# Query loads for two chunks at once, as token pairs in 512-byte rows, with keys turned apart from them

## The chip, the cores and the metric

The kernel runs on one core of one Trainium2 chip. The metric is the device time of one execution in microseconds. Three runs of the kernel before took 303.69, 302.69 and 303.46 us, median 303.46. "PE" in the rows is TensorE, DVE VectorE, ACT ScalarE, POOL GpSimd and SP SyncE, the engine that issues nearly all transfers.

## The reference

A retention layer (attention without softmax, with a decay for each head) feeds a gated feed-forward layer:

```python
# q, k, v: (8 batches, 8 heads, 576 tokens, 64)
scores = matmul(q, k.transpose) / 8
ret = scores * where(row >= col, gamma[head] ** (row - col), 0)
attn = matmul(ret, v)
x = attn.transpose(0, 2, 1, 3).reshape(4608, 512)
gate = sigmoid(x @ w_gate)                # (512, 1536)
out = (gate * (x @ w_val)) @ w_out        # (1536, 512)
```

All inputs and the output are float32; the kernel computes in bfloat16 and sums in float32.

## The kernel before

**Retention by chunks.** The decay is split into a factor of the query's place and one of the key's place, so q and k are scaled by tables (`qtab`, `ktab`) when they are cast to bfloat16. A sequence of 576 tokens is four chunks of 128 tokens and a last one of 64. For a chunk the kernel makes the scores inside it, masks them with the triangle `tri`, multiplies them with v (`intra`), and adds the product of the queries with the running state, the sum of k·v over the chunks before (`inter`). A chunk is worked in two pieces of 64 tokens, `j`. Heads `y*4 + m` lie by halves: `half(y)` is the 64 partitions of one half, `m` one of four positions in a row.

The first six chunks of batches 0 and 1 go through a code of their own (`PAIRS`) that loads two chunks at once as token pairs, in 512-byte rows. The rest are 30 **steps** (`STEPS`), of one chunk each; the last chunks of two batches share a step (6, 11, 20 and 29). `load(s)` issues the loads of k, q and v of a step, in rows of 256 bytes (one head of one token). `cast_qk` scales and casts k and q into one tile `natural_qk[s]`, keys and queries side by side; `cross(s)` turns both by one transposing transfer on SP's queue, and steps 0, 1 and 7 (`TURNED`) are turned on TensorE by `turn_step` instead, with a copy on ACT and one on DVE. `cast_v` makes the values. Scores, state products and values are 64x64 matmuls.

**The feed-forward layer** runs over blocks of columns (tokens): one of 512 for the first pairs, two of 256, then seven of 512. In the blocks of 512 the products are made by a scheme with seven products of quarters for eight, whose operands are sums and differences: of weights (`w_sums`, `wo_sums`), of x (`x_sums`, tile `xsum`) and of the gated values (`gv_sum`, tile `gsum`). These sums run on DVE ("v") or POOL ("p"), as written in the order lists. For this scheme, x lies in the blocks of 512 with even tokens first and odd tokens behind ("dealt"); ACT writes it so from the value banks (`leave_two`, line 788, and line 800).

**Order.** Everything is issued in program order from one list of units: `FIRST`, `ORDER` and `FINAL` are the quarter products of the first, a middle and the last block of 512; a tag such as `0-1v` behind one adds a sum. `LATER*` puts sums beside the products of the output. Between the units, `SUMS_AT` places weight sums, casts (`c`) and turns (`t`) in the form block.unit, `PAIRS_AT` and `next_two` place the bursts of attention, `CASTS_AT` and `LEAD_CAST` the casts of later steps, `AHEAD` says how many steps the loads run ahead of the casts, `EARLY` which gate products of the next block stand among the output products of this one, `SOONER` when stores are issued. `LOOK_ACT`, `K_ON_POOL` and `V_ON_ACT` choose engines by step; from step 11 on (`SCALED_V`) keys are cast without scaling and values are scaled on POOL instead. `CUTS`, `FIRST_OP_CUTS` and `OP_CUTS` say how many 512-column matmuls are issued as two of 256. Each engine works through its own queue in order, SP's queue of transfers too: a transposing transfer there waits for its cast, and the loads behind it with it.

The sum that a DVE row at `L324` shows is a weight sum of the output matrix, `L365` one of gate or value weights, `L829` the addition to the running state, `L658` its cast for the products, `L686` the scores, `L718` and `L734` the value and state products, `L1046` the quarter products, `L1173` and `L1249` those of the output, `L1306` and `L1549` the output of the first three blocks.

Of the kernel before, what the change touches and what calls it, by code (L numbers as in the profile page):

```python
# [16 lines left out]
def kernel(  # L17
# [146 lines left out]

    def load(s):
        b, c = STEPS[s]
        tiles = []
        for nm, src in (("k", k), ("q", q), ("v", v)):
            t = landing([P, H, D], f"{nm}32_{s}", s >= 8)
            if c < LAST:  # L170
                nc.sync.dma_start(out=t, in_=src[b, :, c * P:(c + 1) * P, :].rearrange("h p d -> p h d"))
            else:
                for j, (bj, tj) in enumerate(pieces_of(s)):
                    nc.sync.dma_start(out=t[half(j)], in_=src[bj, :, tj:tj + 64, :].rearrange("h p d -> p h d"))
            tiles.append(t)
        loaded[s] = tiles
# [117 lines left out]
    def later_constants():  # L294

        nc.gpsimd.memset(tri, 1.0)
        for p0 in (0, 64):
            nc.gpsimd.affine_select(out=tri[p0:p0 + 64], in_=tri[p0:p0 + 64], compare_op=ALU.is_ge, fill=0.0,
                                    base=0, pattern=[[1, 64]], channel_multiplier=-1)
# [95 lines left out]

    natural = {}
# [17 lines left out]
    natural_qk = {}  # L414
# [5 lines left out]
    def cast_qk(s, i, eng):  # L420
        c = STEPS[s][1]
        if i == 1:
            natural_qk[s] = nat_pool.tile([P, 2, M, P], BF16, tag="qk", name=f"qk_{s}")
        to = natural_qk[s][:, i].rearrange("p m (y d) -> p y m d", y=2)
        if i == 1 and s >= SCALED_V:
            (on_pool if s in K_ON_POOL else on_act)(out=to, in_=by_halves(loaded[s][0]))
            return
        tab = (qtab, ktab)[i][:, c, :].rearrange("p (y m) -> p y m", y=2).unsqueeze(3).to_broadcast([P, 2, M, D])
        eng.tensor_tensor(out=to, in0=by_halves(loaded[s][1 - i]), in1=tab, op=ALU.mult)  # L429

    SCALED_V = 11
    X_LATE = "ppvp"
    X_FIRST = "vvvp"
    LOOK_ACT = (0, 5, 6, 9, 10, 13, 14, 17, 18, 19, 20, 21, 22, 25, 26, 27, 29, 33, 34)
    K_ON_POOL = (13, 15, 17, 18, 19, 22, 26, 27, 28, 29)
    V_ON_ACT = ()

    def cast_v(s, eng):
        natural["v", s] = nat_pool.tile([P, H, D], BF16, tag="v", name=f"v_{s}", bufs=6)
        if s >= SCALED_V:  # L440
            tab = ktab[:, STEPS[s][1], :].unsqueeze(2).to_broadcast([P, H, D])
            nc.gpsimd.tensor_tensor(out=natural["v", s], in0=loaded[s][2], in1=tab, op=ALU.mult)  # L442
        else:
            eng(out=natural["v", s], in_=loaded[s][2])

    def cross(s):
        t = att_pool.tile([P, 2, M, P], BF16, tag="T", name=f"T_{s}", bufs=6)
        nc.sync.dma_start_transpose(out=t.rearrange("p j m t -> p (j m) t"),
                                    in_=natural_qk[s].rearrange("p j m d -> p (j m d)"))
        turned[s] = t  # L450

    turned = {}

# [24 lines left out]
    def pair_qk(A, g, banks, between=None):  # L478
# [8 lines left out]
        if g == 0:  # L487
            probs["p", A] = [att_pool.tile([P, M, 2, P], BF16, tag="T", name=f"ptp_{A}_{hh}", bufs=6) for hh in range(2)]
# [135 lines left out]
    def turn_step(s):  # L624

        t = att_pool.tile([P, 2, M, P], BF16, tag="T", name=f"T_{s}", bufs=6)
        for i, ((pool, tag), eng) in enumerate(zip(VALS, (on_act, on_dve))):
            ps = pool.tile([P, M, P], BF16, tag=tag, name=f"turn_{s}_{i}")
            for m in range(M):
                nc.tensor.matmul(ps[:, m, :], lhsT=natural_qk[s][:, i, m, :], rhs=ident, is_transpose=True,  # L630
                                 start=(m == 0), stop=(m == M - 1))
            eng(out=t[:, i], in_=ps)
        turned[s] = t
# [47 lines left out]
    def scores(s, begins):  # L681
        t = turned[s]
# [1009 lines left out]
```

## Time and profile before

| | |
|---|---|
| median of three runs | 303.46 us (302.69 to 303.69) |
| profiled execution | 303.89 us, of which the span from first to last instruction 302.2 us |
| TensorE busy | 295.6 us, 98% of the span, granted clock 0.999 |
| weight loads / DVE / ACT / POOL busy | 250.0 / 230.4 / 204.9 / 225.8 us |
| DMA | 54.99 MB in 146,464 packets, 124,400 of them under 512 bytes |
| transfers on SP's queue, as a share of 16 engines | 73.6% |

The busy share of an engine is an average over the whole span. What bounds a stretch is read from the chain of work that ended last, which is followed back from the last instruction: at each step to what released it, or to the instruction before it on its engine. Matmuls overlap, and their ends are modelled, so a row's mean length (273 ns for 256 columns) is longer than the distance between two of them.

### The profile page before, as it was taken

How to read it: one execution, taken by the hardware profiler on the slowest of the kernel's cores; microseconds unless marked ns; L12 is line 12 of the kernel's file. 1: busy time of each engine (PE TensorE's matmuls, PEld its weight loads, DVE VectorE, ACT ScalarE, POOL GpSimd, SP SyncE). 2: the span in 40 equal slices, each digit the busy share in tenths (PEclk: the TensorE clock that was granted, in tenths of full speed). 3: DMA queues.
4: the chain of work that ended last, by engine and by line, in shares of the span. 5: the costliest groups of instructions: out<-in, count | busy, mean ns of one | idle time of the engine just before them, and what ended most of it. 6: DMA issues, size and time to landing. Idle time of an engine off the chain costs nothing.

```text
span 302.2 us, 10696 instructions
## 1 busy us (share of the span) xinstructions
PE 295.6 (98%) x4437; PEld 250.0 (83%) x4437; DVE 230.4 (76%) x439; ACT 204.9 (68%) x414; POOL 225.8 (75%) x253
## 2 busy tenths in 40 slices
PE   7999999999999999999999999999999999999994
PEld 3677876978868888888888888888888888888883
DVE  5967895796986998789748974896489848935893
ACT  6755565335369657985798589857985698559830
POOL 5775854846669888978997898789978946860780
PEclk9999999999999999999999999999999999999999
DMA  7999999979998989999749967976694165004013
GB/s 205 336 370 379 322 334 229 210 160 202 213 175 184 257 173 196 219 201 262 141 108 199 259 143 155 218 185 143 124 204 132 37 123 193 4 2 139 3 36 104
DMA packets 146464, 54.99 MB, mean 182 GB/s; under 512 B 124400, under 2 KB 139760, under 8 KB 146416
## 3 DMA queue, kind: packets, MB, share of 16 engines
q1 hardware_dynamic: 145328, 53.59, 73.6%
q8 instruction: 34, 0.56, 0.8%
q10 hardware_dynamic: 1088, 0.72, 0.8%
q14 instruction: 14, 0.11, 0.1%
HBM read 37.75 MB, written 9.44 MB: 156 GB/s over the span
## 4 chain that ended last, share of the span: by engine, by line
PE 92%; DVE 2%; DMA 2%; issue 1%; ACT 1%; POOL 0%; SPq 0%; DVEq 0%
PE gatea L1046 12%; PE wa L1046 11%; PE qa L1173 11%; PE qe L1173 9%; PE gatee L1046 6%; PE we L1046 5%; PE op L1549 4%; PE h_v L886 3%; PE h_g L886 3%; PE gateg L1046 3%; PE wg L1046 3%; PE hv L1374 3%; PE op L1306 3%; PE val L718 2%; PE qa L1249 2%; PE hg L1374 2%
## 5 line engine op out<-in xcount | busy, mean ns | idle before, releaser
L1046 PEld LDWEIGHTS <-wg_sb 128*128 128x128 bf16 x348 | 34.1, 98 | 4.1
L1073 POOL TENSOR_TENSOR gv<-gv,wu 128x512 bf16<-128x512 bf16 x20 | 23.5, 1174 | 15.5 <-DVE wu L1085 15.4
L1173 PEld LDWEIGHTS <-gsum 128*128 128x128 bf16 x312 | 30.0, 98 | 3.7
L429 POOL TENSOR_TENSOR qk<-q,qtab 128x512 bf16<-128x512 f32 x28 | 30.3, 1082 | 3.5 <-DMA q<-in_q_dram 3.5
L1046 PEld LDWEIGHTS <-wv_sb 128*128 128x128 bf16 x296 | 28.9, 98 | 3.6 <-issue 0.2
L1085 DVE TENSOR_TENSOR gu<-gatee,gu 128x512 f32<-128x512 f32 x22 | 15.2, 690 | 19.4 <-ACT gateg L1077 10.2
L943 POOL TENSOR_TENSOR gsum<-gsum,gv 128x256 bf16<-128x256 bf16 (+1 forms) x20 | 17.6, 890 | 14.4 <-DVE gsum L943 12.6
L1046 PEld LDWEIGHTS <-wgt_sb 128*128 128x128 bf16 x264 | 25.8, 98 | 3.0
L1046 PE MATMUL gatea<-xsum,wg_sb 128*128 128x256 bf16 x172 | 25.6, 273 | 0.0
L1173 PEld LDWEIGHTS <-gv 128*128 128x128 bf16 x228 | 21.8, 98 | 2.7
L1088 DVE TENSOR_TENSOR gs<-gatea,gs 128x512 f32<-128x512 f32 x22 | 15.2, 689 | 9.5 <-PE gatea L1046 9.4
L943 POOL TENSOR_TENSOR gsum<-gv,gsum 128x256 bf16<-128x256 bf16 (+1 forms) x24 | 21.9, 922 | 0.2
L429 POOL TENSOR_TENSOR qk<-k,ktab 128x512 bf16<-128x512 f32 x11 | 11.6, 1054 | 13.4 <-DMA k<-in_k_dram 13.2
L704 DVE TENSOR_TENSOR pt<-row,tri 128x512 bf16<-128x512 f32 x30 | 19.2, 680 | 2.8 <-PE row L686 2.6
L442 POOL TENSOR_TENSOR v<-v,ktab 128x512 bf16<-128x512 f32 x19 | 20.9, 1101 | 0.0
L1046 PE MATMUL wa<-xsum,wv_sb 128*128 128x256 bf16 x136 | 20.4, 273 | 0.1
L658 ACT CAST sb<-s 128x512 bf16<-128x512 f32 (+1 forms) x26 | 14.3, 569 | 8.8 <-DVE s L829 8.7
L788 ACT CAST xT<-val 128x512 bf16<-128x512 f32 x26 | 14.7, 592 | 7.0 <-PE val L734 7.0
L943 DVE TENSOR_TENSOR gsum<-gv 128x512 bf16<-128x512 bf16 (+1 forms) x34 | 19.1, 589 | 0.0
L1046 PEld LDWEIGHTS <-wvt 128*128 128x128 bf16 x168 | 16.4, 98 | 1.9
L943 POOL TENSOR_TENSOR gsum<-gv 128x256 bf16<-128x256 bf16 (+1 forms) x20 | 17.6, 882 | 0.0
L1071 ACT ACTIVATE gv<-gs 128x512 bf16<-128x512 f32 x22 | 13.9, 633 | 5.4 <-DVE gs L1088 5.4
(210 smaller groups left out, 883.9 us busy)
## 6 DMA issues: line engine op xcount, KB each, us to landing
k<-in_k_dram SPq DMA_DIRECT2D x26, 256.0 KB, 3.9
q<-in_q_dram SPq DMA_DIRECT2D x26, 256.0 KB, 4.2
v<-in_v_dram SPq DMA_DIRECT2D x26, 256.0 KB, 4.6
out_dram<-ob SPq DMA_DIRECT2D x24, 256.0 KB, 2.7
wg<-in_moe_w_gate_dram SPq DMA_DIRECT2D x12, 256.0 KB, 5.4
wv<-in_moe_w_val_dram SPq DMA_DIRECT2D x12, 256.0 KB, 5.6
wo<-in_moe_w_out_dram SPq DMA_DIRECT2D x12, 256.0 KB, 5.6
v32p<-in_v_dram SPq DMA_DIRECT2D x6, 256.0 KB, 4.5
```

The lines of the kernel that those rows point to most:

```text
L429: eng.tensor_tensor(out=to, in0=by_halves(loaded[s][1 - i]), in1=tab, op=ALU.mult)
L442: nc.gpsimd.tensor_tensor(out=natural["v", s], in0=loaded[s][2], in1=tab, op=ALU.mult)
L704: nc.vector.tensor_tensor(out=t[:, y, 0:n].rearrange("p i m t -> p (i m) t"), in0=rows_tile[ss[0]][y][:, 0:n].rearrange("p i m t -> p (i m ...
L788: nc.scalar.copy(out=to, in_=src)
L886: nc.tensor.matmul(ps[:, i], lhsT=w_sb[:, kc, (fc + i) * P:(fc + i + 1) * P], rhs=xT(kc, slice(t0, t0 + n)), start=(kc == 0), stop=(kc == ...
L943: eng.tensor_tensor(out=to, in0=a, in1=b, op=op)
L1046: nc.tensor.matmul(ps[:, f], lhsT=w[:, kc, f * P:(f + 1) * P], rhs=x[:, kc], start=(first and f == 0 and kc == 0), stop=(f == 1 and kc == ...
L1073: eng.tensor_tensor(out=to, in0=to, in1=src[:, part], op=ALU.mult)
L1085: nc.vector.tensor_tensor(out=me["u2"], in0=e, in1=me["u2"], op=ALU.add)
L1088: nc.vector.tensor_tensor(out=me["s5"], in0=a, in1=me["s5"], op=ALU.add)
L1173: nc.tensor.matmul(ps[:, b], lhsT=left(fp)[:, b * P:(b + 1) * P], rhs=right(fp), start=(first and fp == 0 and b == 0), stop=(fp == NFC // ...
L1374: nc.tensor.matmul(ps[:, cols], lhsT=(wg_sb if what == "g" else wv_sb)[:, kc, fc * P:(fc + 1) * P], rhs=xT(kc, cols), start=(kc == 0), sto ...
```

## The change

Queries of steps with a whole chunk are loaded for two chunks (256 tokens) by the first step of the two, `opens(s)`, as two tiles of four heads each. A row of a tile holds two neighbouring tokens, 512 bytes. They are scaled by the pair tables (`qtab2`) into one tile of 8 times 128 columns, turned by one transposing transfer (or, for steps 0 and 7, eight transposes), and used by both steps. Keys get tiles of their own and are turned alone, by half the transfer of before.

```diff
+    def opens(s):
+        return STEPS[s][1] < LAST and STEPS[s][1] % 2 == 0
     def load(s):
...
+            if nm == "q" and opens(s):
+                for g in range(2):
+                    t = landing([P, M, 2, D], f"q32_{s}_{g}", s >= 8)
+                    nc.sync.dma_start(
+                        out=t.rearrange("p h r d -> p h (r d)"),
+                        in_=q[b, g * M:(g + 1) * M, c * P:(c + 2) * P, :].rearrange("h (p r) d -> p h (r d)", r=2))
+                    loaded["q", s, g] = t
+            elif nm != "q" or c == LAST:
+                t = loaded[nm, s] = landing([P, H, D], f"{nm}32_{s}", s >= 8)
...
+    def cast_k(s, eng):
+        natural_k[s] = nat_pool.tile([P, M, P], BF16, tag="nk", name=f"nk_{s}", bufs=6)
...
+    def cast_q(s, engs):
+        if c < LAST and not opens(s):
+            return
+        natural_q[s] = nat_pool.tile([P, 2, M, P], BF16, tag="nq", name=f"nq_{s}", bufs=2)
...
+        for g in range(2):
+            tab = qtab2[:, c // 2, g * M:(g + 1) * M, :].unsqueeze(3).to_broadcast([P, M, 2, D])
+            engs[g].tensor_tensor(out=natural_q[s][:, :, :, half(g)].rearrange("p r m d -> p m r d"),
+                                  in0=loaded["q", s, g], in1=tab, op=ALU.mult)
...
     def cross(s):
-        nc.sync.dma_start_transpose(out=t.rearrange("p j m t -> p (j m) t"),
-                                    in_=natural_qk[s].rearrange("p j m d -> p (j m d)"))
+        nc.sync.dma_start_transpose(out=turned_k[s], in_=natural_k[s].rearrange("p m d -> p (m d)"))
+        if q_ is not None and STEPS[s][1] == LAST:
+            nc.sync.dma_start_transpose(out=q_[:, 0], in_=natural_q[s][:, 0].rearrange("p m d -> p (m d)"))
+        elif q_ is not None:
+            nc.sync.dma_start_transpose(out=q_.rearrange("p r m t -> p (r m) t"),
+                                        in_=natural_q[s].rearrange("p r m d -> p (r m d)"))
```

Since even and odd tokens of a chunk now lie apart in the turned queries, a piece of 64 queries is read as two runs of 32 columns, and scores, mask and values keep the order "32 even, 32 odd". The mask `tri` and the reads of the value banks follow from that; in the blocks of 512 the copy to x no longer sorts even from odd, in the blocks of 256 it now mixes them.

```diff
+    def q_of(s, y, m, j):
+        return turned_q[s][half(y), :, m, j * 32:j * 32 + 32]
...
-                    nc.tensor.matmul(row_ps[s][y][half(j), m, :], lhsT=t[half(y), 1, m, half(j)],
-                                     rhs=t[half(y), 0, m, half(j)], ...
+                    nc.tensor.matmul(row_ps[s][y][half(j), m, :].rearrange("p (r t) -> p r t", r=2),
+                                     lhsT=turned_k[s][half(y), m, half(j)], rhs=q_of(s, y, m, j), ...
...
     def turn_step(s):
-        for i, ((pool, tag), eng) in enumerate(zip(VALS, (on_act, on_dve))):
+        sides = [(turned_k[s], natural_k[s], on_dve)]
+        if q_ is not None:
+            sides.insert(0, (q_.rearrange("p r m t -> p (r m) t"), natural_q[s].rearrange("p r m d -> p (r m) d"), on_act))
...
-        src = vals_tile[vals[0]][j].rearrange("p (i m) (t r) -> p i m r t", i=2, r=2)
+        src = vals_tile[vals[0]][j].rearrange("p (i m) (r t) -> p i m r t", i=2, r=2)
```

The tiles take the same room as before: 6 key and 2 double query tiles for 5 double ones, 4 turned key tiles and 4 double turned tiles for 6 double ones.

The order lists are set anew:

```diff
-    X_LATE = "ppvp"
-    X_FIRST = "vvvp"
-    LOOK_ACT = (0, 5, 6, 9, 10, 13, 14, 17, 18, 19, 20, 21, 22, 25, 26, 27, 29, 33, 34)
-    K_ON_POOL = (13, 15, 17, 18, 19, 22, 26, 27, 28, 29)
-    V_ON_ACT = ()
+    X_LATE = 'pvvp'
+    X_FIRST = 'vpvp'
+    LOOK_ACT = (0, 5, 6, 10, 13, 14, 15, 17, 18, 19, 20, 21, 22, 26, 27, 28, 29, 30, 33, 34)
+    K_ON_POOL = (13, 15, 17, 18, 19, 22, 27, 29)
+    V_ON_ACT = (12,)
...
-    AHEAD = (2, 2, 1, 1, 0, 1, 1, 0, 1, 2, 1, 1)
+    AHEAD = (2, 2, 1, 1, 0, 1, 1, 2, 2, 3, 2, 1)
...
-    EARLY = ((11, "g01"), (13, "g05"))
-    CASTS_AT = (13, 34)
+    EARLY = ((10, 'g01'), (13, 'g05'))
+    CASTS_AT = (9, 36)
...
-    LATER_FIRST = {0: ('2a3p', '2b3p'), 4: ('1-4v',), 9: ('2a4p', '2b4p')}
+    LATER_FIRST = {1: ('2a3p',), 2: ('2b3v',), 3: ('1-4p',), 7: ('2a4v',), 10: ('2b4p',)}
...
-    LATER = {0: ('2-1v',), 1: ('1-2v', '2-2p'), 2: ('2-3p',), 4: ('1-3v',), 9: ('1-4p',), 10: ('2-4p',)}
+    LATER = {0: ('2-1v', '1-2v'), 2: ('2-2p',), 4: ('2-3p', '1-3v'), 9: ('1-4p',), 10: ('2-4p',)}
...
-    OP_CUTS = (6, 11, 0, 0)
+    OP_CUTS = (4, 11, 0, 0)
...
-    CUTS = 60
+    CUTS = 62
...
-    FIRST_OP_CUTS = 20
+    FIRST_OP_CUTS = 18
...
-    SUMS_AT = ("0.0:c03p 0.1:f00p 0.3:g00p 0.3:w10v 0.3:w11v 0.6:t01p 0.7:o10p 0.8:c02v "
-               "0.9:o00v 0.11:c05p 0.11:c07p 0.12:w13v 0.12:c06v 0.14:g01v 0.14:g03p 1.0:o20v "
...
+    SUMS_AT = ("0.1:c03p 0.2:f00p 0.3:w10v 0.3:w11v 0.5:g00v 0.7:o00v 0.7:t01p 0.8:c02v 0.9:c07p 0.10:c06v "
+             "0.10:w13v 0.11:c05p 0.13:c04p 0.14:o10v 0.15:g01v 1.0:o20v 1.0:o01v 1.2:g03p 1.3:o11p 1.5:o03v "
...
-    PAIRS_AT = ((0, 10), (0, 11), (1, 10), (1, 0))
+    PAIRS_AT = ((0, 10), (0, 9), (1, 10), (1, 2))
...
-    SOONER = (-14, -21, 12)
+    SOONER = (-16, -22, 10)
```

`FIRST`, `ORDER`, `FINAL` and `LATER_FINAL` change in a few places: single products trade neighbouring positions, and some sums hang on another product.

More of the change, by code (lines that the diff above doesn't have):

```diff
@@ L487, in pair_qk @@
         if g == 0:
-            probs["p", A] = [att_pool.tile([P, M, 2, P], BF16, tag="T", name=f"ptp_{A}_{hh}", bufs=6) for hh in range(2)]
+            probs["p", A] = [att_pool.tile([P, M, 2, P], BF16, tag="T", name=f"ptp_{A}_{hh}", bufs=4) for hh in range(2)]
         for hh in range(2):
@@ L624, in turn_step @@
     def turn_step(s):
-        t = att_pool.tile([P, 2, M, P], BF16, tag="T", name=f"T_{s}", bufs=6)
-        for i, ((pool, tag), eng) in enumerate(zip(VALS, (on_act, on_dve))):
[L628 to L633, printed above, removed]
+        q_ = turned_tiles(s)
+        sides = [(turned_k[s], natural_k[s], on_dve)]
+        if q_ is not None:
+            sides.insert(0, (q_.rearrange("p r m t -> p (r m) t"), natural_q[s].rearrange("p r m d -> p (r m) d"), on_act))
+        for i, ((to, of, eng), (pool, tag)) in enumerate(zip(sides, VALS)):
+            n = of.shape[1]
+            ps = pool.tile([P, n, P], BF16, tag=tag, name=f"turn_{s}_{i}")
+            for m in range(n):
+                nc.tensor.matmul(ps[:, m, :], lhsT=of[:, m, :], rhs=ident, is_transpose=True,
+                                 start=(m == 0), stop=(m == n - 1))
+            eng(out=to, in_=ps)
     running = {}
```

106 lines of the change are left out of this document (61 added, 45 removed), and 2 rows, old and new, of the table SUMS_AT.

## The prediction

> **What bounds the kernel now.** I read the busy shares first, then the engines' busy time by stage, then the chain that ended last, and only then the transfers that the change is about.
>
> ```profile
> PE 295.6 (98%) x4437; PEld 250.0 (83%) x4437; DVE 230.4 (76%) x439; ACT 204.9 (68%) x414; POOL 225.8 (75%) x253
> ...
> 0.00:10.00 10.00, 7.96 (x68) 3.65 (x69) 6.87 (x28) 6.12 (x11) 5.57 (x15) 1.00 0.81 235
> 10.00:20.00 10.00, 9.45 (x186) 7.36 (x186) 8.23 (x16) 6.40 (x14) 7.47 (x13) 1.00 1.11 355
> 60.00:70.00 10.00, 9.93 (x257) 7.89 (x255) 8.68 (x18) 4.36 (x10) 4.48 (x6) 1.00 0.86 187
> 100.00:110.00 10.00, 9.95 (x161) 8.17 (x161) 9.96 (x17) 5.09 (x12) 8.28 (x8) 1.00 0.99 238
> 150.00:160.00 10.00, 10.00 (x94) 8.97 (x92) 5.42 (x11) 9.09 (x19) 9.52 (x11) 1.00 0.58 132
> 290.00:300.00 10.00, 8.27 (x76) 7.13 (x73) 6.50 (x14) 1.88 (x5) 4.43 (x4) 1.00 0.29 92
> ```
>
> In the second view the columns behind the stretch are its length, then PE, weight loads, DVE, ACT and POOL, each with its count, then granted clock, DMA share and GB/s. TensorE is busy 98% of the span, at full clock. Of the 6.6 us that it is not busy (302.2 - 295.6), the front holds 2.04 + 0.55, the stretch from 290 to 300 holds 1.73, and the last 2.2 us are the drain. Neither front nor end is touched by the change, apart from two order lists near the end. In the middle only two stretches are below 10.00, by 0.07 and 0.05 us. A busy TensorE can still be waiting, so the chain is needed:
>
> ```profile
> 60.79 0.69 DVE gv L891
> 61.48 1.19 DVE wt_sb L324
> ...
> 65.95 0.41 ACT sb L658
> ...
> 66.41 0.25 PE val L734 x6
> 66.66 0.25 PE row L686 x31
> ...
> 100.49 0.96 DVE gsum L943
> ...
> 103.35 0.04 issue
> 103.39 0.60 PE wa L1046 x4
> ...
> 138.25 1.31 PE qa L1173 x12
> ...
> 168.47 1.31 PE qa L1173 x12
> ...
> 198.74 1.31 PE qa L1173 x12
> ...
> 228.87 1.31 PE qa L1173 x12
> ...
> 259.32 1.31 PE qa L1173 x12
> ```
>
> The columns are start, length and what held the chain. It leaves TensorE in the middle at only two places: around 61 to 66 us a queue of DVE work ends in a state copy on ACT that the value products wait for, and around 100 to 103 us DVE is late. From 138 us on, the same piece of each block of 512 tokens recurs after 30.27, 30.13 or 30.45 us (30.22 for the first). Twelve matmuls in 1.31 us are 109 ns each, and 94 in the 10 us from 150 are 106. So the steady part is a plain stream of matmuls. No row of the chain after the first pairs is a load.
>
> **What can be won at all.** A matmul whose end is modelled covers part of a gap, so a gap is the idle time plus what a last matmul is shown too long: at 66 us 0.07 plus 0.19 (below), some 0.26; at 103 us 0.05 plus 0.27 - 0.11, some 0.21. If every late block took the shortest period, 0.09 + 0.14 + 0.32 more would go. Together 1.0 us of 302, and that needs every stall gone. A change of 0.3%, 0.9 us, is about what a measurement of this kernel can tell from none.
>
> **The change, part by part.**
>
> ```profile
> L686 PE MATMUL row<-T 64*64 64x64 bf16 x480 | 7.3, 196 | 0.0
> L734 PE MATMUL val<-T,sb 64*64 64x64 bf16 x368 | 10.7, 195 | 0.1
> L1046 PE MATMUL wa<-xsum,wv_sb 128*128 128x256 bf16 x136 | 20.4, 273 | 0.1
> ...
> 82.00 1.73 PE op L1306 x8
> 83.73 0.45 PE turn L630 x8
> ...
> 85.29 0.06 PE val L734 x8
> ...
> 85.55 0.29 PE row L686 x31
> ```
>
> Turning on TensorE: steps 0, 1 and 7 now cost 8 transposes each, 24 in all. After it, step 0 turns 4 key tiles and 8 of a query pair, step 1 only 4 (its queries came with step 0), step 7 again 12. That is 28, four more at 0.45/8 = 0.056 us, on the bounding engine: +0.22 us. The cuts of wide matmuls (60 to 62, 20 to 18, and 6 to 4 in the first block) take two away in sum. A cut makes two of 0.109 out of one of 1.73/8 = 0.216 us, so two fewer are worth 0.004 us: nothing.
>
> The second cost hangs on ACT. Step 7 is turned just ahead of a burst of attention:
>
> ```profile
> 83.67 0.62 ACT L658 CAST sb<-s 128x512 bf16<-128x512 f32 x1 [1.51 <-DVE s L829]
> 84.20 0.58 ACT L632 COPY T<-turn 128x512 bf16<-128x512 bf16 x1
> 84.68 0.41 ACT L658 CAST sb<-s 128x256 bf16<-128x256 f32 x1
> ...
> 85.31 0.24 PE L734 MATMUL val<-T,sb 64*64 64x64 bf16 x8
> ```
>
> The copy of the turned queries now moves 1,024 columns. The same engine's casts of 256 and 512 columns take 0.41 and 0.62 us, so 256 columns add 0.21; two such steps on top of 0.58 make an estimated 1.0 us, and the copy's end moves from 84.8 to 85.2. Behind it in ACT's order stands the state cast, which moves from 85.09 to 85.5. The products that read it start at 85.31 plus the 0.22 of extra turning, 85.53. I take +0.1; the ends are 0 and the copy's whole growth, 0.43. [...]
>
> Transfers: queries of two chunks come as two pieces of 256 KB with 512 bytes a row in place of two with 256 bytes. The number of loads and bytes stays; 13 pairs are loaded so.
>
> ```profile
> DMA packets 4001, 1.99 MB, mean 331 GB/s; under 512 B 120, under 2 KB 4001, under 8 KB 4001
> ...
> DMA packets 8068, 2.05 MB, mean 228 GB/s; under 512 B 8067, under 2 KB 8067, under 8 KB 8067
> ...
> 59.98 1.88 SPq L448 DMA_TRANSPOSE T<-qk  x1
> ...
> L448 SPq DMA_TRANSPOSE T<-qk x27: 1232/1697/4111, 55.5 to 244.0; - x27
> ...
> DMA to landing us min/median/max: 2.7/4.2/6.1
> ```
>
> The first line is the transfers from 6 to 12 us, nearly all of 512 bytes or more; the second those from 46 to 55 us, all of 256 bytes. A pair's 0.52 MB takes 1.6 us at the one rate and 2.3 at the other: 0.7 saved thirteen times, 9 us of transfer time. It is hidden, as the chain shows no load. Against it stand more transposing transfers on SP: 27 for keys, 11 for pairs, 4 for the odd last chunks, 42 in place of 27, though with fewer tiles (27x4 + 11x8 + 4x4 = 212 for 216). If each costs SP its 1.7 us whatever its size, SP gains 25 us of work over some 190; if cost goes by tiles, none. The tightest user is steps 2 and 3: their last transpose is issued at 59.98 and lands about 4.2 later, at 64.2, and the scores start at 66.66, 2.5 us of slack. One more transpose at 1.7 us still fits, and before the last key tile of the two the same five tiles must land as now. I take 0; if the slack breaks, rival 1 shows what is late next.
>
> Casts: the queries still cost two scalings of 512 columns per pair of chunks, the keys one each; only their grouping changes. Two key casts leave POOL for ACT (28 and 26; 27 and 29 were and stay). One of the sums of x goes from POOL to DVE in each late block, one from DVE to POOL in the first; two sums of weights go to DVE before 66 us. The first gate product of the next block stands half a product, 0.65 us, earlier, and ACT's casts of x are done ahead of it by about that. The list of value casts on ACT changes nothing, since step 12 goes to POOL anyway, nor do the new pair places, as each pair still waits for the three leftovers of the one before. The longer of the DVE sums, 1.19 us on the chain at 61.48, moves from unit 9 to unit 7, ahead of the queue: I take the 66 us gap as gone, -0.26. For the 103 us gap I take half, -0.1, between 0 and -0.21: one sum of x leaves DVE some 10 us ahead of it, but the long sum at 100.49 stays.
>
> Sum: +0.22 + 0.1 - 0.26 - 0.1 = -0.04 us. The profiled execution took 303.89 us (302.2 span and 1.7 around it) and becomes 303.85. It lies 0.43 above the median of the three runs, 303.46, which becomes 303.4.
>
> **The rivals.** 1: DVE becomes late, which ends slower.
>
> ```profile
> 61.39 1.27 DVE L324 TENSOR_TENSOR wt_sb<-wo_sb 128x512 bf16<-128x512 bf16 x1
> ...
> L970 DVE TENSOR_TENSOR xsum<-xT,xsum x7: 410/898/1357, 89.2 to 269.9; 128x512 bf16<-128x512 bf16 x7
> ...
> 183.57 0.69 DVE L1085 TENSOR_TENSOR gu<-gatee,gu 128x512 f32<-128x512 f32 x1 [2.70 <-ACT gateg L1077]
> ```
>
> A DVE sum of this shape takes 0.41 us at its shortest and 1.36 at its longest. If the moved sum lands late in each of the six late blocks and the queue behind it delays the additions that free TensorE's banks, the price is up to 6 x 0.95 = 5.7 us; at a third of it, 303.4 + 1.9 = 305.3. It decides once DVE's lag exceeds its idle time at that place, and the 2.70 us that it idles after the sums at 183 speak against. The 0.21 us gap at 103, where DVE is busy 9.96 of 10, speaks for. [...]
>
> 2: all stalls go, and the late copy costs nothing: 303.46 + 0.22 - 1.0 = 302.7. The wide loads speak for it, the chain without a load against.
>
> 3: the moving operand of scores and of the state products is now two runs of 32 columns instead of one of 64. By the rows above, 31 scores take 0.29 us (9.4 ns each) and 8 state products 0.06 (7.5). Doubled for 480 and 432 that is 4.5 + 3.2 = 7.7 us, up to 311. [...]
>
> 4: the wide pieces aren't faster than the narrow ones. Then no transfer time is won and the time is that of the forecast, since it was hidden.
>
> **How the numbers follow.** Forecast 0.55 (rival 4 with it, 0.05 of these), rival 1 0.24, rival 2 0.16, rival 3 0.05. The likeliest alone reaches from 302.9 (both gaps gone, no late copy, half of the periods' spread) to 304.3 (copy at 0.43, both gaps stay, and 0.2 of new stalls). The range runs from 302.4, 0.3 below rival 2 for the scatter of the runs, to 305.3, which takes in rival 1 at a third. Faster by over 0.3%, under 302.55: a third to half of rival 2 and a tail of the forecast, 0.14. Slower, over 304.4: most of rival 1 and rival 3, 0.27. The rest, 0.59, within.
>
> **What would show it.** Right: 4,439 matmuls within a few; 42 transposing transfers; query issues with 512-byte rows; fewer packets under 512 bytes by some 27,000; still no load on the chain after 15 us; periods near 30.2 us; the piece at 66 us on TensorE. Wrong: a chain that leaves TensorE for DVE sums of x or g in several late blocks (rival 1), scores above 9.4 ns each (rival 3), or a gap at the burst after step 7's turning well over 0.1.

## The result and the profile after

Slower: 307.66 us (median of 6 runs, 305.8 to 308.87) beside 303.61 of the kernel before on the same chip (6 runs, 302.69 to 305.03), a ratio of 1.0129 with an interval of 1.0094 to 1.0165. That is outside the range, which ended at 305.3. The ratios, here and below, are estimated from all fast runs and are not the quotients of the medians. The profiled execution took 307.59 us, with a span of 305.9 (302.2 before).

The page of the changed kernel, and its chain of waits by engine; the last line is the same row of before:

```profile
PE 297.6 (97%) x4437; PEld 250.7 (82%) x4437; DVE 230.0 (75%) x450; ACT 205.8 (67%) x417; POOL 215.1 (70%) x239
...
DMA packets 133120, 54.86 MB, mean 179 GB/s; under 512 B 97744, under 2 KB 126416, under 8 KB 133072
...
PE 77%; DMA 7%; SPq 5%; POOL 5%; issue 2%; DVE 1%; ACT 1%; DVEq 0%
```
```profile
PE 92%; DVE 2%; DMA 2%; issue 1%; ACT 1%; POOL 0%; SPq 0%; DVEq 0%
```

No engine has more work worth naming: POOL has 10.7 us less. Of TensorE's 2.0 us more, the four further transposes are 0.2; the rest are mostly two groups with as many matmuls as before, of nearly the same length, that now stand further apart. What changed is the chain. Before, TensorE held 92% of it; now 77%, and DMA, SP's queue (`SPq`) and POOL, 2% together before, hold 17%. The time lost is mostly waiting, and the busy time by stage says where. Three stretches of the changed kernel (columns as in the prediction), then the one of before that the prediction did not show:

```profile
60.00:70.00 10.00, 10.00 (x256) 7.83 (x254) 8.04 (x18) 4.46 (x10) 3.60 (x4) 1.00 0.89 165
...
100.00:110.00 10.00, 8.99 (x78) 7.40 (x77) 9.45 (x16) 5.11 (x9) 8.42 (x8) 1.00 0.84 212
...
180.00:190.00 10.00, 9.79 (x89) 8.48 (x87) 4.80 (x12) 8.38 (x19) 8.25 (x9) 1.00 0.81 173
```
```profile
180.00:190.00 10.00, 10.00 (x94) 8.97 (x93) 5.33 (x10) 9.45 (x20) 8.13 (x9) 1.00 0.67 145
```

The 66 us gap is gone, as forecast. The one at 103 us, which the prediction halved, grew to a full microsecond, and TensorE is starved again at 180 to 190. The waits from 98 to 106 us name the first, and the chain leads back from it. First the wait (us in total, times, longest) and the chain of the changed kernel (start, length, what held it), then the row of DVE where it waits for POOL:

```profile
PE wa L1100 <- DVE ws L1142: 1.0, 1, 1.0
```
```profile
75.60 0.17 SPq L499
...
75.81 4.25 DMA k<-in_k_dram
...
80.14 1.05 POOL nk L446
81.19 0.82 SPq L501
...
85.26 4.75 DMA q<-in_q_dram
...
90.38 1.47 POOL nq L459 x2
...
99.36 2.25 POOL gv L1127 x2
...
101.63 1.37 DVE gsum L997
...
104.21 0.69 DVE ws L1142
...
104.94 0.60 PE wa L1100 x4
```
```profile
101.63 1.36 DVE L997 TENSOR_TENSOR gsum<-gv 128x512 bf16<-128x512 bf16 x1 [0.49 <-POOL gv L1127]
```

Read it backwards. TensorE waits for a sum on DVE, which stands behind a gated-value sum, which waits for a product that POOL started at 99.31 (its row is below) and before at 97.77. POOL's casts waited for loads, and SP issued those loads behind transposing transfers (`L499`, `L501`). Between the casts and the gated products POOL also has more to do than before: two sums of x and two of weights.

```profile
93.13 1.33 POOL L1024 TENSOR_TENSOR xsum<-xT 128x512 bf16<-128x512 bf16 x1
94.42 1.15 POOL L1024 TENSOR_TENSOR xsum<-xT,xsum 128x512 bf16<-128x512 bf16 x1
95.53 1.15 POOL L375 TENSOR_TENSOR wg_sb<-wg_sb 128x512 bf16<-128x512 bf16 x1
96.64 1.16 POOL L375 TENSOR_TENSOR wv_sb<-wv_sb 128x512 bf16<-128x512 bf16 x1
...
99.31 1.17 POOL L1127 TENSOR_TENSOR gv<-gv,wu 128x512 bf16<-128x512 bf16 x1
```

The same engine before has one of each there:

```profile
92.72 1.41 POOL L970 TENSOR_TENSOR xsum<-xT,xsum 128x512 bf16<-128x512 bf16 x1
94.10 1.15 POOL L365 TENSOR_TENSOR wv_sb<-wv_sb 128x512 bf16<-128x512 bf16 x1
...
97.77 1.16 POOL L1073 TENSOR_TENSOR gv<-gv,wu 128x512 bf16<-128x512 bf16 x1
```

POOL comes to these sums 0.41 us later (93.13 for 92.72) and needs 6.18 us for 5.05 from there to the gated product: two sums more, one query cast fewer. Of the 1.54 us that the product is late, 0.41 come from ahead of the sums and 1.13 from the work between. So there are two candidates, and the chain runs through both: SP's transposing transfers (the data path), and two sums of 1.15 to 1.33 us put on POOL (the order lists: the second place of `X_FIRST`, a sum of x, and `g22`, a sum of gate weights). What a transfer costs SP, in rows of one line each (shortest, median, longest in ns):

```profile
L499 SPq DMA_TRANSPOSE kT<-nk x27: 1195/1571/3117, 54.0 to 245.8; - x27
...
L503 SPq DMA_TRANSPOSE qT<-nq x11: 1231/1239/2483, 56.7 to 227.4; - x11
...
L501 SPq DMA_TRANSPOSE qT<-nq x4: 1188/1206/2412, 80.8 to 247.1; - x4
```

`L499` moves four tiles of 128x128, `L503` eight, `L501` four, and the combined transfer of before eight: all take 1.19 to 1.23 us at the shortest. At their shortest eight tiles take 0.04 us more than four, so nearly all of that price comes with the issue and not with the bytes; what stretches a row to 3.1 us, the profile doesn't name.

### The profile page after: what moved, and what is told of

It reads as the page before. It is cut to its first block, busy times and chain, and to the rows that moved or that the text cites. A ratio compares the mean times of both kernels' runs of the same rounds, so it can differ in the third digit from the quotient of the medians.

```text
span 305.9 us, 10725 instructions
## 1 busy us (share of the span) xinstructions
PE 297.6 (97%) x4437; PEld 250.7 (82%) x4437; DVE 230.0 (75%) x450; ACT 205.8 (67%) x417; POOL 215.1 (70%) x239
## 4 chain that ended last, share of the span: by engine, by line
PE 77%; DMA 7%; SPq 5%; POOL 5%; issue 2%; DVE 1%; ACT 1%; DVEq 0%
PE gatea L1100 11%; PE wa L1100 10%; PE qa L1227 9%; PE qe L1227 7%; PE gatee L1100 5%; PE we L1100 5%; PE op L1603 3%; PE hv L1428 3%; SPq L195 3%; PE h_g L940 3%; PE gateg L1100 2%; PE wg L1100 2%; DMA k<-in_k_dram 2%; PE h_v L940 2%; DMA wg<-in_moe_w_gate_dram 2%
## 5 line engine op out<-in xcount | busy, mean ns | idle before, releaser
L446 POOL TENSOR_TENSOR nk<-k,ktab 128x512 bf16<-128x512 f32 x11 | 11.5, 1049 | 20.5 <-DMA k<-in_k_dram 18.9
L459 POOL TENSOR_TENSOR nq<-q,qtab 128x512 bf16<-128x512 f32 x24 | 24.9, 1059 | 0.4 <-POOL nk L446 0.4
L997 POOL TENSOR_TENSOR gsum<-gv,gsum 128x512 bf16<-128x512 bf16 (+1 forms) x24 | 22.9, 968 | 0.2
L997 DVE TENSOR_TENSOR gsum<-gv 128x512 bf16<-128x512 bf16 (+1 forms) x40 | 20.9, 545 | 0.5 <-POOL gv L1127 0.5
L473 POOL TENSOR_TENSOR v<-v,ktab 128x512 bf16<-128x512 f32 x19 | 20.1, 1060 | 0.0
L1127 POOL TENSOR_TENSOR gv<-gv,ws 128x512 bf16<-128x512 bf16 x14 | 16.3, 1165 | 2.7 <-DVE ws L1142 2.3
L1125 ACT ACTIVATE gv<-gu 128x512 bf16<-128x512 f32 x22 | 14.2, 646 | 5.7 <-DVE gu L1139 5.7
```

The costliest lines, as they stand in the source:

```text
L459: engs[g].tensor_tensor(out=natural_q[s][:, :, :, half(g)].rearrange("p r m d -> p m r d"), in0=loaded["q", s, g], in1=tab, op=ALU.mult)
L473: nc.gpsimd.tensor_tensor(out=natural["v", s], in0=loaded["v", s], in1=tab, op=ALU.mult)
L997: eng.tensor_tensor(out=to, in0=a, in1=b, op=op)
L1127: eng.tensor_tensor(out=to, in0=to, in1=src[:, part], op=ALU.mult)
```

## The experiments

In the expectations, a "gap" is the distance between the starts of two matmuls beyond the length of the first; it can be some 0.2 us more than the idle time in a row. Ratios are to the kernel before on the same chip; its medians there were 303.8 to 304.5 us.

**1. Each half alone.** The new data path with every order list as before, and the old data path with every list as after (both from `X_LATE` to `SOONER`; nothing else is touched).

> The new way of loading and turning, with all order lists as they were before. Theory SP (the 15 further transposing transfers, each at SP's fixed price of about 1.2 us, hold up the loads behind them): still slow, 306 to 309 us. Theory orders (the new lists put two sums more on POOL ahead of the gate products at 93 to 99 us, and DVE and TensorE wait for POOL): within 0.3% of 303.6 us, and the gap of 1.17 us at 104 us is 0.3 or less.

> The old way of loading and turning, with all the new order lists. Theory SP: within 0.5% of 303.6 us. Theory orders: 306 to 308 us, with a gap of about 1 us on TensorE near 104 us.

Measured: the data path alone 306.53 us, ratio 1.007 (1.0044 to 1.0097); the lists alone 306.95 us, 1.0084 (1.0045 to 1.0122). Each half is slower by itself, so neither theory holds alone. The runs of the lists alone spread from 304.98 to 309.43 us, and the profiled one, 305.07, is among the shortest, so its rows show less than the median lost. The halves starve TensorE in different places. The first row is the data path alone, the second and third the lists alone:

```profile
180.00:190.00 10.00, 8.53 (x80) 7.49 (x78) 4.07 (x8) 7.99 (x18) 9.64 (x11) 1.00 1.01 207
```
```profile
100.00:110.00 10.00, 8.64 (x101) 6.94 (x101) 9.38 (x15) 4.17 (x9) 8.43 (x8) 1.00 0.70 180
...
180.00:190.00 10.00, 10.00 (x94) 8.95 (x93) 5.34 (x12) 9.69 (x21) 7.71 (x8) 1.00 0.70 148
```

The gap at 103 us belongs to the lists, the one past 180 to the data path. How much is lost where can be read from the start of the first score in the same bursts of attention (us):

| | step 7's burst | near 110 | near 145 | near 175 | near 200 | last burst | end of span |
|---|---|---|---|---|---|---|---|
| before | 85.38 | 109.61 | 145.14 | 175.35 | 200.39 | 260.96 | 302.2 |
| changed | 85.68 | 111.16 | 147.11 | 177.92 | 203.55 | 264.12 | 305.9 |
| data path alone | 85.66 | 109.86 | 145.55 | 176.47 | 203.16 | 263.64 | 304.8 |
| lists alone | 84.49 | 110.11 | 145.64 | 175.92 | 201.13 | 261.61 | 303.4 |

Against the kernel before, the changed one loses 0.30 us by step 7's burst, 1.25 more around 103 us, 0.42 more by 145, 0.60 more by 175, 0.59 more by 200, nothing in the blocks up to 261, and 0.5 at the end. Losses from 110 to 200 appear with the data path alone; those around 103 and at the end appear with the lists alone. The end is clear in every profile: from the first score of the last burst it takes 41.1 to 41.2 us in all nine profiles with the old lists there and 41.5 to 41.8 in all nine with the new ones. Which list does it was not tested.

**2. The price of an issue on SP.** The kernel before, each of its 27 transposing transfers cut into two of four tiles; keys first; bytes and casts unchanged.

```diff
-        nc.sync.dma_start_transpose(out=t.rearrange("p j m t -> p (j m) t"), in_=...)
+        for i in (1, 0):
+            nc.sync.dma_start_transpose(out=t[:, i], in_=natural_qk[s][:, i]...)
```

> The kernel before, with each of its 27 transposing transfers cut in two, keys first and then queries: 54 issues, the same tiles. Theory SP: each further issue costs SP about 1.2 us, 27 x 1.2 = 32 us more on its queue, so loads and casts come late and the time is 306 to 310 us. Theory orders: SP has room, within 0.3% of 303.6 us.

Measured: 309.11 us, ratio 1.0168 (1.0136 to 1.0199), 5.3 us for 27 more issues. Half the tiles did not halve the price of an issue: it is 1.19 us at the shortest where it was 1.23, and 1.24 in the median where it was 1.70. TensorE was starved in both stretches in which the changed kernel is, and most of all at 80 to 90 us, where the changed kernel is not:

```profile
L449 SPq DMA_TRANSPOSE T<-qk x54: 1188/1237/2442, 55.9 to 249.7; - x54
```
```profile
80.00:90.00 10.00, 7.65 (x236) 4.81 (x226) 5.92 (x14) 4.49 (x9) 5.46 (x7) 1.00 1.09 177
...
100.00:110.00 10.00, 9.13 (x81) 7.67 (x79) 8.97 (x14) 6.50 (x13) 8.44 (x8) 1.00 0.73 184
...
180.00:190.00 10.00, 9.27 (x155) 8.20 (x142) 5.84 (x13) 7.83 (x18) 9.49 (x10) 1.00 0.72 135
```

SP had little room for them: adding up SP's rows in the timeline of the kernel before, its issues take 90.0 of the 100 us from 30 to 130 (92.0 in the changed kernel). The prediction never added them up. Two limits of this sum: a load of 256 KB holds SP for 0.38 us in one row and 3.06 in another, so part of it may be waiting that the profile doesn't explain; and the 16 DMA engines are about as full there (a share of 0.83 to 1.26 in the stretches of 10 us). Their busy time on this queue was 222 us before, 219 in the changed kernel and 232 in the split one. So the changed kernel did not give them more to do, but the 5.3 us of the split one price the issue and 10 us more of their work together.

**3. The two sums back on DVE.** In the changed kernel, and in the old data path with the new lists:

```diff
-    X_FIRST = 'vpvp'
+    X_FIRST = 'vvvp'
...
-    ... 2.1:g22p ...
+    ... 2.1:g22v ...
```

> The changed kernel, with two sums put back from POOL to DVE: the second sum of x in the first block of 512 and the gate weights' third sum at 2.1. Theory orders: POOL comes 1.3 + 1.15 us sooner to the gated products at 99 us, the gap of 1.17 us at 104 us falls under 0.3, and the time to some 306 us. Theory SP: POOL waits for the late loads instead, the gap and the time stay (307 to 308 us).

> The old data path with the new order lists (before_new_orders: 306.95 us, ratio 1.0084, with a TensorE gap of 1.52 us at 102.5 us), except that two sums go back from GpSimd to VectorE: the second of the four sums on X_FIRST and g22 of block 2. Orders theory: those two sums of 1.2 to 1.3 us each stand on GpSimd ahead of the gated products, so without them the gap at 102.5 us goes and the time falls by about 1.5 us, to 305.4 or less, ratio 1.000 to 1.004. Rival, the lists as a whole are at odds with the old path: the gap moves to another place between 80 and 110 us as it did in after_pool_relief, and the time stays within 0.7 us of 306.95.

Measured: on the old path 304.59 us, ratio 1.0033 (1.0008 to 1.0058), 0.5% below the 1.0084 with the sums on POOL. So these two sums are probably most of what the lists cost; the comparison is across two chips, the intervals overlap between 1.0045 and 1.0058, and the profiled execution, 307.61 us, is the longest of its twelve and loses 1.66 us at 90 to 100, so its rows decide nothing. On the new path 306.8 us, 1.0085 (1.0057 to 1.0114): the gap at 103 us went (last row below), but TensorE now loses 0.49 and 0.65 us in the two stretches ahead. In two later executions with the same two sums on DVE (`relief_k23` below) it loses at most 0.17 us from 80 to 110, so the gap at 103 us does not come back when TensorE is on time.

```profile
80.00:90.00 10.00, 9.51 (x209) 5.98 (x204) 7.85 (x16) 5.21 (x10) 8.64 (x9) 1.00 1.19 224
90.00:100.00 10.00, 9.35 (x84) 8.01 (x83) 8.23 (x13) 8.70 (x18) 8.77 (x9) 1.00 0.90 209
100.00:110.00 10.00, 10.00 (x90) 8.55 (x89) 9.94 (x17) 5.98 (x11) 7.97 (x8) 1.00 0.90 223
```

**4. The gap past 180 us.** In the new path with the old lists, ACT waits for a load. The chain, SP's queue and ACT of a second execution of that kernel (`oldord_again`):

```profile
178.48 0.21 SPq L501
...
178.74 4.56 DMA k<-in_k_dram
...
184.25 0.49 ACT gateg L1131
...
184.78 0.27 PE gateg L1100
```
```profile
176.19 1.20 SPq L499 DMA_TRANSPOSE kT<-nk  x1
177.49 1.20 SPq L501 DMA_TRANSPOSE qT<-nq  x1
178.74 1.77 SPq L182 DMA_DIRECT2D k<-in_k_dram  x1
```
```profile
183.32 0.62 ACT L444 CAST nk<-k 128x512 bf16<-128x512 f32 x1 [1.92 <-DMA k<-in_k_dram]
183.85 0.40 ACT L712 CAST sb<-s 128x256 bf16<-128x256 f32 x1
184.15 0.58 ACT L1131 COPY gateg<-gatea 128x512 f32<-128x512 f32 x1
```

Step 20 now has two transposing transfers where it had one; the first starts at 176.19, when the casts of its keys (on ACT) and queries (on POOL) have ended, and the second behind it. The keys of step 23 are loaded behind both; ACT's cast of those keys stands ahead of the copies that free TensorE's gate banks, and TensorE waits 1.4 us for the copy that ACT starts at 184.15. Two ways to take that away, neither with more work for any engine:

```diff
-    K_ON_POOL = (13, 15, 17, 18, 19, 22, 26, 27, 28, 29)
+    K_ON_POOL = (13, 15, 17, 18, 19, 23, 26, 27, 28, 29)      # oldord_k23
```
```diff
-    AHEAD = (2, 2, 1, 1, 0, 1, 1, 0, 1, 2, 1, 1)
+    AHEAD = (2, 2, 1, 1, 0, 1, 1, 0, 1, 2, 1, 1) + (2,) * 8 + (3,)      # oldord_ahead
```

> The changed data path with all the old order lists (after_old_orders: 306.53 us, profiled execution 306.7, its one large TensorE gap 1.63 us at 182 us), but the key cast of step 23 goes to GpSimd and that of step 22 to ScalarE: one cast each, so neither engine has more to do. Late-load theory: in after_old_orders ScalarE waits 2.01 us for the load of step 23's keys, which SP can issue only behind the transposes of step 20, and the copies of the gate products queue behind that cast. With the cast elsewhere the wait goes, the gap at 182 us falls from 1.63 to under 0.3 us and the time by about 1.3 to 1.6 us, to 304.9 to 305.2 (ratio to the kernel before about 1.004). Rival, a general shortage of SP time: the lateness shows elsewhere (GpSimd then waits for the same load, and its sums come late), the gap only moves, and the time stays at 306 to 306.8.

> The changed data path with all the old order lists, but the four loads of step 23 (keys, two query pieces, values) are issued with those of step 22, ahead of step 20's two transposes on SP instead of behind them. Late-load theory: the keys of step 23 land some 8 us sooner, ScalarE does not wait 2.01 us for them, the gap of 1.63 us at 182 us goes, and the time falls by 1.3 to 1.6 us to about 305.0, as in oldord_k23. If both that kernel and this one do it, the late load ahead of the gate copies is the cause. Rival, shortage of SP time: four loads at 0.58 us are put ahead of the transposes of step 20, those come 2.3 us later, and a gap of 0.5 to 1.5 us opens where the scores of step 20 or 21 wait for them; time 306 to 307.

> The changed data path with all the old order lists once more, beside the same kernel with the key cast of step 23 on GpSimd. Late-load theory: the gap of about 1.6 us at 182 us is there again, and the time is 1.0 to 1.6 us above oldord_k23_again. If the two are within 0.4 us, the gap at 182 us was a matter of one execution, and the cost of the data path lies elsewhere.

> The same kernel as oldord_k23 (305.24 us, ratio 1.0058). Late-load theory: no gap at 182 us, ratio to the kernel before 1.003 to 1.006, 1.0 to 1.6 us below oldord_again. What is left over the kernel before should be the 0.3 us of step 7 and small gaps between 80 and 95 us, where SP is busy nine tenths of the time.

Measured: `oldord_k23` 305.24 us, 1.0058 (1.0031 to 1.0084), and `oldord_ahead` 305.53 us, 1.0043 (1.0026 to 1.0061). Side by side on one chip, `oldord_again` 306.8 us, 1.0086 (1.0057 to 1.0116), and `oldord_k23_again` 305.5 us, 1.0047 (1.0024 to 1.007). The intervals overlap (1.0057 to 1.007), and across the two chips of the first comparison the ratios differ by only 0.1 to 0.3%. But TensorE lost 1.4 to 1.5 us in this stretch in both executions with the late cast (8.63 of 10 in `oldord_again`, 8.53 in the row of experiment 1) and nothing without it, by either way:

```profile
180.00:190.00 10.00, 10.00 (x95) 8.96 (x93) 5.44 (x11) 9.70 (x21) 9.64 (x10) 1.00 0.96 211
```

That is the row of `oldord_k23_again`. The traces tell more than the times here, because the two executions of one kernel differ mostly ahead of the first score: it started at 62.93 us in `oldord_k23` and at 61.23 in `oldord_k23_again`, though the kernel is the same. From the first score to the end of the span the two executions with the late cast took 243.2 and 243.3 us, the two without it 241.7 and 241.8, the one with the loads ahead 242.0, and the kernel before 240.7. So the late load explains 1.2 to 1.5 of the 2.5 us that the data path costs by itself in the traces, about half of it by the ratios on one chip.

**5. The rest of the data path: more issues, or fewer.** On `oldord_k23`, each of the 11 transfers of a query pair cut into two; and step 7's query pair turned by SP, not by TensorE.

```diff
-            nc.sync.dma_start_transpose(out=q_..., in_=natural_q[s]...)      # oldord_k23_qsplit
+            for r in range(2):
+                nc.sync.dma_start_transpose(out=q_[:, r], in_=natural_q[s][:, r]...)
```
```diff
             if x not in TURNED:
                 cross(x)
+            elif x == 7:      # oldord_k23_q7; turn_step(7) turns the keys alone
+                nc.sync.dma_start_transpose(out=turned_tiles(x)..., in_=natural_q[x]...)
```

> oldord_k23 with each of the 11 transposing transfers of a query pair (8 tiles) cut into two of 4 tiles: 53 issues for 42, the same bytes. SP theory (a fixed price of 1.2 us for each issue, and no room on SP): 13 us more of SP, and by the price of the kernel before, 5.3 us for 27 more issues, about 11/27 x 5.3 = 2.2 us, to about 307.4, with new gaps between 75 and 110 us and near 180 us. Rival, cost by tiles: nothing changes, 304.8 to 305.7.

> oldord_k23 with the query pair of step 7 turned by one transposing transfer on SP, and only its keys on TensorE: eight transposes of 0.056 us fewer, 0.45 us, and the 0.1 us of the late copy on ScalarE, for one issue of 1.2 us more on SP near 75 us. If TensorE's own work is the price there, it gains 0.4 to 0.5 us, to 304.8. SP theory: the issue pushes the loads behind it by 1.2 us in the stretch that has no room, gaps between 80 and 105 us grow by 0.5 to 1.2 us, and the time is 305.2 to 306.

Measured: 307.04 us, 1.0102 (1.0055 to 1.0149), for 11 more issues, 1.5 us over `oldord_k23_again` in the same comparison where 2.2 was expected over the 305.24 of the first; but its six runs lie from 305.33 to 309.48 and the intervals overlap, so this agrees and does not prove. The trade at step 7 is even: 305.63 us, 1.0043 (1.002 to 1.0067). Eight transposes of TensorE were saved, and in the profiled execution TensorE lost more than that in the stretches around:

```profile
80.00:90.00 10.00, 9.37 (x182) 6.05 (x175) 8.23 (x18) 4.86 (x10) 6.77 (x8) 1.00 1.14 208
...
100.00:110.00 10.00, 9.34 (x120) 7.65 (x121) 9.90 (x16) 4.68 (x9) 8.45 (x8) 1.00 0.98 261
```

The opposite trade was made on the changed kernel with all its lists: the keys of steps 3 and 5 on TensorE, two transfers fewer on SP.

```diff
-    TURNED = (0, 1, 7)
+    TURNED = (0, 1, 3, 5, 7)
...
+    0.12:t03v ... 1.6:t05v ...
```

> The changed kernel, with the key transposes of steps 3 and 5 done on TensorE (eight transposes of 0.056 us more, 0.45 us) instead of on SP (two of 1.2 us or more less, in the crowded stretch from 60 to 90 us). SP theory (a fixed price of 1.2 us per transfer on an SP that has no room): the loads behind them come 1.2 to 2.4 us sooner, GpSimd waits less for keys (18.9 us now), and the gaps at 94 and 104 us (0.21 and 1.17 us) fall to under 0.4 us together: 307.66 + 0.45 - 1.0 = about 307.1. Orders theory (the gap at 104 us comes from two more sums on GpSimd ahead of the gated products): the gap stays within 0.3 us of 1.17, and the time goes up by the 0.45 us to about 308.1.

Measured: 307.59 us, 1.0106 (1.0069 to 1.0142). Neither number was met, but the rows tell them apart:

```profile
70.00:80.00 10.00, 9.27 (x88) 8.16 (x86) 6.99 (x12) 3.80 (x7) 6.52 (x8) 1.00 0.94 193
80.00:90.00 10.00, 9.13 (x276) 6.13 (x276) 8.43 (x18) 5.09 (x9) 8.92 (x10) 1.00 1.00 245
90.00:100.00 10.00, 10.00 (x89) 8.57 (x88) 7.67 (x12) 8.79 (x18) 7.10 (x7) 1.00 1.12 206
100.00:110.00 10.00, 9.95 (x89) 8.55 (x89) 9.42 (x17) 6.54 (x12) 7.78 (x7) 1.00 0.58 120
```

The gap at 103 us is gone although both sums are still on POOL. With two transfers fewer on SP, POOL began the two sums of x at 89.38 us, not at 93.13, and stood idle for 1.96 us ahead of the gated product. So either remedy takes this gap away: fewer issues ahead, or fewer sums on POOL. It does not need the new transfers, since the lists alone made it on the old path. What was won there was lost ahead of it: TensorE waited for a product on DVE and for a copy behind it, 0.7 and 0.8 us. One copy of turned keys, 0.41 us, stands ahead of that product among DVE's weight sums; that the copies are the cause is not shown.

**6. All known causes away, and the wide pieces priced.** The changed kernel with both sums on DVE and the key cast of step 23 on POOL in place of step 22's, twice; with the loads of step 23 ahead as well; and with the query loads in 256-byte pieces, one for the even tokens of all heads and one for the odd.

```diff
-                    t = landing([P, M, 2, D], f"q32_{s}_{g}", s >= 8)
+                    t = landing([P, H, D], f"q32_{s}_{g}", s >= 8)      # relief_narrow
...
+                        out=t, in_=q[b, :, c * P:(c + 2) * P, :].rearrange("h (p r) d -> p h r d", r=2)[:, :, g])
```

> The changed kernel with two sums back on VectorE (after_pool_relief: 306.8 us; it has no gap at 103 us but 0.58 us in two at 185 to 188 us, 0.98 at 90 to 92 and 0.65 at 83), and with the key casts of steps 22 and 23 exchanged between ScalarE and GpSimd. Late-load theory: the two gaps at 185 to 188 us go, the time falls by 0.4 to 0.6 us to about 306.3; the earlier gaps at 83 and 90 us, which come from SP's early queue, stay. Rival: no change, 306.6 to 307.0.

> The same kernel as relief_k23, beside the others on one chip and with more rounds: 305.0 to 305.7 us, ratio to the kernel before 1.003 to 1.007, so still slower than the kernel before. What is left over it by the profile: 0.22 us of four transposes more on TensorE and 0.1 at step 7, and about 0.6 us near 172 us.

> relief_k23 with the loads of step 23 issued together with those of step 22, ahead of step 20's transposes. The key cast no longer stands ahead of the gate copies, so the late-load theory expects nothing more from it: within 0.4 us of relief_k23 (305.3). If SP's order there still costs something, the gaps from 172 to 188 us shrink and it gains 0.3 to 0.6 us, to about 304.8. Only a gain above 1.2 us would bring it under the kernel before, which neither theory expects.

> As relief_k23 (305.34 us), the same issues, casts and transposes, but each two-chunk query load takes its tokens in 256-byte pieces: one load for the even tokens of all eight heads and one for the odd, in place of one for each half of the heads in 512-byte pieces. It prices the wide pieces alone. If the wide pieces pay, the query loads land later here (12 x 2 loads of 256 KB), GpSimd waits longer for queries and keys, and the time goes up by 0.5 us or more, to 305.8 to 307. If, as the constant 0.58 us of SP per load whatever its pieces suggests, the price lies in the issue and not in the bytes, the time stays within 0.4 us of relief_k23.

Measured: 305.34 us, 1.0059 (1.0031 to 1.0087), then 306.42 us, 1.0093 (1.006 to 1.0126); with the loads ahead 307.14, 1.0101 (1.0072 to 1.0129); narrow 306.54, 1.0082 (1.0052 to 1.0111). Misses: the kernel did not repeat its 305.3, so a difference of 0.3% between kernels of this family can't be claimed, and by these times the cast of step 23 is not shown to help. The traces show it: between the bursts at 175 and 200 us both executions take 25.06 us, as the kernel before (25.04), where `after_pool_relief` took 25.68. Two thirds of the 0.9 us between the spans of the two executions lie ahead of the first score. And no cost of the narrow loads is shown: 306.54 against 306.42 in one comparison, where a third of a per cent could hide. The loads' medians of time to landing (last number, us) differ by 0.3, but a wide kernel, `oldord_k23_again`, has 4.6 too. First the narrow kernel, then the wide one:

```profile
q<-in_q_dram SPq DMA_DIRECT2D x26, 256.0 KB, 4.6
```
```profile
q<-in_q_dram SPq DMA_DIRECT2D x26, 256.0 KB, 4.3
```

The narrow loads did hold SP longer, 0.92 us in the median of 26 rows where the wide ones took 0.57 and the same was expected of both, and the time did not show it. So these 0.35 us more in each row of SP were not time added to the kernel, where the one late load of experiment 4 cost 1.2 to 1.5 us.

No version beat the kernel before.

## Why the prediction was wrong, point by point

- **Bound and ceiling.** TensorE bounded the kernel before, with 92% of the chain; that held. No version gained, so the ceiling of 1.0 us was not tested.
- **Four more transposes, +0.22 us: held**, 28 of them in the trace. **ACT's larger copy at step 7, +0.1: held.** It took 1.01 us where 1.0 was estimated. The term takes it that the state cast waits behind the copy, and it did: the cast started at 85.11 us, and at 84.68 before, 0.43 earlier. The burst started 0.30 us later than before, where the two terms together gave 0.32.
- **The 66 us gap gone: held**; 10.00 of 10.
- **The transposing transfers, "I take 0": the step that failed, for some 1.6 of the 3.7 us.** (These are the losses from 110 to 200 us, which come with the data path alone.) The prediction had both bounds, "if each costs SP its 1.7 us whatever its size, SP gains 25 us". That was the true branch, at 1.2 us at the shortest (15 more issues, 18 us). Two errors followed. I tested slack at one place only, steps 2 and 3, where it existed; I did not add up SP's own queue, which was occupied for nine tenths of the time from 30 to 130 us. And I asked only whether the turned tiles came in time, not what stands behind the transfers on SP: the next loads, then POOL's and ACT's casts, then sums and copies. The gap past 180 us hangs on those: step 23's keys came late, ACT's cast of them held the copies behind it, and the cast or the load moved took the gap away. "No load on the chain" became a chain with 7% DMA and 5% SP's queue.
- **The 103 us gap, -0.1: the second failing step, 1.25 us lost in place of 0.1 won.** I counted the move of a sum of x off DVE as relief and did not count it on the queue that got it. With `g22` it put two sums, some 2.5 us, on POOL ahead of the gated products, and DVE waited for those. The gap became a microsecond.
- **The end, "neither front nor end is touched by the change, apart from two order lists near the end": the third step that failed.** These lists got no term, and the end takes 0.5 us longer with the new lists, on the old data path too.
- **Wide pieces, 9 us of transfer time saved, hidden: held.** The DMA engines' time on this queue was 223 us with narrow query loads and 213 to 219 in three executions with wide ones, 4 to 10 us less, and no gain in time is shown. Packets under 512 bytes fell by 26,656 (forecast 27,000).
- **Rivals.** The first had the sign and the symptom, a late DVE, and the wrong cause and place: DVE was late because POOL was, and at 103 us only, not in the six late blocks. The second, all stalls gone, is refuted: only the one at 66 us went. The third, scores from two runs of columns, is refuted: at step 7's burst 32 scores take 0.28 us from the first start to the next group's, and took 0.29 before. The fourth gives the forecast's time and is told apart only by the transfer time, which did fall.

Both halves were 0.7 to 0.8% alone and 1.3% together. What is still open: 0.4 to 0.6% of the data path without its late load (`oldord_k23`, `oldord_ahead`). The 0.3 us of step 7 is part of it, and trading that for one more issue gains nothing; small gaps near 150 and 172 us, 0.2 to 0.5 us each, have no releaser in the profile, so that SP's issues cause them too is not shown.

## What to carry to other kernels

Add up the queue that issues transfers by stage, as one adds up an engine: here an issue of 1.2 us looked cheap beside the 4.2 us until its transfer landed and counted on a queue that was nine tenths full (90.0 of 100 us), and one transfer split into two of half the size paid the price of an issue twice (1.23 us at the shortest before, 1.19 for each half). The sum says where to look, not what the time will be: here that was decided by the engine behind the late load, 1.4 to 1.5 us of TensorE past 180 us with the cast on ACT and nothing with it on POOL. When work moves to another engine, count it on the engine that receives it, and follow what is queued behind it until an engine is reached that can wait. That a gap goes with one change does not show that the other had no part: a chain can be shortened at more than one place. Undoing each half alone shows which half makes the gap. And where executions differ ahead of the change, compare the times between the same two events in the traces.

## What the runs showed of the hardware

A transposing transfer from SBUF to SBUF held SP for 1.19 to 1.23 us at its shortest, whether it moved four tiles of 128x128 or eight, and for up to 4.1 in the kernel before. A plain load of 256 KB held it for 0.38 us at the shortest, with rows of 512 bytes (queries of the changed kernel) and of 256 (keys of both). In the median it was 0.57 to 0.58 with rows of 512 bytes; with rows of 256 it was 0.58 for the keys, 1.20 for the values of the kernel before and 0.58 for those of the changed one, and 0.92 for the queries of `relief_narrow`. In the kernel before, the stretch from 6 to 12 us, nearly all in rows of 512 bytes and more, moved 331 GB/s, and the one from 46 to 55, in rows of 256, gave 228; no gain in time from that is shown here.

In the traces of both kernels work behind a late row came late with it. In the kernel before, a transposing transfer started on SP at 86.92 us, as POOL's cast of its queries ended (86.89), held SP for 4.11 us, and the next load started at 91.08. ACT's state cast started at 84.68 us behind a copy of 0.58 us that started at 84.20, and in the changed kernel at 85.11 behind one of 1.01 us that started at 84.20; neighbouring rows overlap by 0.1 us in these profiles.
